# Accumulating DMAs from GpSimd, column-tiled projections and earlier Q steps in a kernel of softmax and linear attention

## The chip, the cores and the metric

The kernel runs on one core of one Trainium2 chip. The metric is device time in microseconds. Three runs of the kernel before gave 707.06, 707.91 and 708.15 us, median 707.91. Profiles come from one further execution of each kernel. Engine names are those of the profile: PE is TensorE, ACT is ScalarE, DVE is VectorE, POOL is GpSimd, SP is SyncE, PEld is the loading of weights into TensorE.

## What is computed

The input `x` has 2048 rows of 512 columns. Branch A is softmax attention with 32 heads of 16 columns, branch B is linear attention with the same sizes, and a gate mixes them by row:

```python
qkv = x @ wqkv                                   # each branch has its own weights
# A, for each of 32 heads
p = softmax(q @ k.T * 16**-0.5);  a = (p @ v) @ wo_A
# B
pq, pk = phi(q), phi(k)                          # phi(t) = where(t > 0, t + 1, exp(t)) + 1e-6
b = ((pq @ (pk.T @ v)) / (pq @ sum(pk) + 1e-6)) @ wo_B
g = sigmoid((x * gate_w).sum(-1))
out = g * a + (1 - g) * b
```

Nearly all of the time goes into A: 32 heads x 2048 x 2048 exponentials.

## The kernel before

**Rounds and units.** The 32 heads are four groups of eight (`t8`), the 2048 queries four chunks of 512 (`qc`). A pair of both is worked in two rounds, even heads and odd heads, so there are 32 rounds of four heads. A unit is one head's scores of 128 keys against 512 queries: one matmul with 32 rows (`Qpad`, `KT`, row tiles of TensorE), whose result fills one PSUM bank. A round has 16 key blocks x 4 heads = 64 units, the kernel 2048.

**ScalarE's way.** Two or three units make a score group. Their matmuls (L1821) fill up to three banks, and one exponential (L1836, on ACT) turns them into probabilities in the buffer `PT`. Two sets of three banks take turns, so TensorE fills one while ScalarE empties the other. The values are then gathered by matmuls with 32 columns (`pv_cols`, L1235): four of them, one per head and column tile, are a set and add to the accumulator's bank.

**VectorE's way.** VectorE takes over some units ("claims", L1417). It reads the bank (L1430), shifts the score into an integer of 16 bits, and these bits, read as a float of 16 bits, are a rough power of two. Three such patterns, shifted by the constants in `STEPS` (0, 342, 683) and weighted by `WEIGHTS`, add up to an approximation of the exponential. Up to four units share a buffer of `DP` and are a bundle. When it is full (`close_tri`, `try_close`, L1440 to L1461), VectorE writes the two further patterns into two further buffers of `DP`, one addition of 128x2048 each (L1461). The weights stand in scaled copies of V, kept for key blocks from `KB2` on (L831). A claimed unit thus costs 686 ns of VectorE for its bank, a quarter of two additions, and three matmuls of values instead of one.

**The rest.** Projections for Q, K and V (`proj_pieces`, L745; `step_Q`, L793), all of branch B (`step_M` L908 and its neighbours), the output projections (`out_fns` L1015, `step_pre` L1035, `step_out` L1061) are "steps" in chains, each cut into pieces of two matmuls. A step of Q ends in eight DMAs of 16 KB from `Qs` into `Qpad` (`fill_q`, L781), issued by SP.

**What sets the order.** A planner in Python writes the order when the kernel is built. It keeps an estimated clock for each engine, with durations written down as constants, and places one score group after another (L1775 on). Between two groups it puts sets of values, a piece of a step that is due (`misc_step`, L1614; a step's `target` is counted in three units of ScalarE's way), or a claim; where TensorE would idle, it adds a warm-up matmul on zeros (`fill`, L1639). `MARGIN` is how far ahead of ScalarE a score group is to be ready. A change of TensorE's tiling (row tiles, column tiles, whole array) counts as `SWITCH_T` (L569). Every engine works its list strictly in order and waits on semaphores of the engine or DMA that it depends on. The last round gathers its values in another way, with probabilities as the stationary operand (52 columns a matmul).

Of the kernel before, what the change touches and what calls it, by code (L numbers as in the profile page):

```python
# [17 lines left out]
STATS = {}  # L18
# [10 lines left out]
WEIGHTS = (1.0, 203 / 256, 161 / 256)  # L29
STEPS = (0, 342, 683)  # L30
NG4 = len(STEPS)
# [22 lines left out]
HINT_AT = 150  # L54
KB2 = 10

# [144 lines left out]
def bass_gated_mix__mha_block__linear_attn_block__prompt_kernel(  # L201
# [20 lines left out]
    NPT = 20  # L222
    NB = 13
    NQS = 4
# [4 lines left out]
    KV0, KV1 = 1.0, 1.2  # L229
    PRE_T = 3  # L230
    PRE_GAP = 6
    OUT_GAP = 6

    with ExitStack() as es:
# [52 lines left out]
        xn0 = PT[:, 9 * 512:9 * 512 + 4 * D].rearrange("p (b c) -> p b c", b=4)  # L287
        NTU = 512 * NTRI

        DP = SB([128, NB, NTU], BF16, "DP")  # L290
# [65 lines left out]
        out_counts = [0] * NOUTT  # L356
        semQ = [SEM(f"s_q{i}") for i in range(NQS)]
        q_counts = [0] * NQS

# [136 lines left out]
        def pump(now, look=0.25):  # L496
            try_close()
            while items and DV.t <= now + look:
# [12 lines left out]
                if best[2] > now + look + WAIT_BANK:  # L511
                    return
                emit_item_op(best[1])
# [91 lines left out]
        def f_mm(o, l, r, start=True, stop=True, sg=False):  # L605
            return lambda: nc.tensor.matmul(o, lhsT=l, rhs=r, start=start, stop=stop, skip_group_check=sg)  # L606

        def f_tr(o, i):
            return lambda: nc.tensor.transpose(o, i, identb[:])  # L609
# [108 lines left out]
        def run_piece(b, piece, first):  # L718
            fns, reads, dur, mac = piece
            pe_macro(fns, reads=reads, writes=[r_bank[b]], dur=dur, mac=mac)  # L720

# [186 lines left out]
        def step_M(c, **kw):  # L908

            rd = [r_xcol[c % 2]] + phi_res  # L910

            def pieces(b):
                o = bank_ap(b)
                fns = [f_mm(o, xcol[c % 2][:, tb, :], phi_of(tb)[0], start=(tb == 0), stop=(tb == NTB - 1)) for tb in range(NTB)]
                return [(fns[j:j + 2], rd, 2 * MM512, 2 * MM512) for j in range(0, NTB, 2)]
# [98 lines left out]

        def out_fns(o, tb, which, last=True):  # L1015
            fns = []
            for n, (kind, i) in enumerate(which):
                l = OT[:, i, 128 * tb:128 * (tb + 1)] if kind == "A" else obt(tb)[:, i, :]
                fns.append(f_mm(o, l, (woA if kind == "A" else woB)[:, i, :], start=(n == 0), stop=(last and n == len(which) - 1)))
            return fns  # L1020
# [14 lines left out]
        def step_pre(k, last=True, **kw):  # L1035
            tb = 4 * (NQC - 1) + k
            rd = [r_OT[t][NQC - 1] for t in range(NT8 - 1)] + [r_OBT[tb], r_woA, r_woB, r_g]

            def pieces(b):
                fns = out_fns(bank_ap(b), tb, order_out[:-1], last=last)  # L1040
                return [(fns[j:j + 2], rd, len(fns[j:j + 2]) * MM512, len(fns[j:j + 2]) * MM512) for j in range(0, 7, 2)]
# [19 lines left out]
        def step_out(tb, **kw):  # L1061
# [3 lines left out]
            def pieces(b):  # L1065
                fns = out_fns(bank_ap(b), tb, order_out)
                return [(fns[k:k + 2], rd, 2 * MM512, 2 * MM512) for k in range(0, 8, 2)]

# [159 lines left out]

        PT_URGENT = 12

# [4 lines left out]
        def pv_cols(now, r, force, want, most, least):  # L1235
# [59 lines left out]
        def pv_step(now, force=False, want=None, most=3, least=4):  # L1295

            r = acc_round[0]
            if r >= NR:
# [83 lines left out]

        MIN_LEFT = 14
        MIN_LEFT_LAST = 20
# [24 lines left out]
        def free_buffers():  # L1409

            used = [e[3] for e in pv_pending]
            held_ = [c[0] for c in (tri[0], closing[0]) if c is not None]
            free = [i for i in range(NB) if i not in held_ and not any(x.pend or x in used for x in r_DP[i])]
            free.sort(key=lambda i: max(x.tr for x in r_DP[i]))
            return free

        def claim(r, u, b, beside, in_group=False):  # L1417
            taken[r].add(u)
            if tri[0] is None:
                ntri[0] += 1  # L1420
                tri[0] = (free_buffers()[0], [])
# [15 lines left out]
        def add_products(i, z, k, r, u):  # L1437
            pv_pending.append((r, u, [(DP[:, i, 512 * k:512 * (k + 1)].bitcast(F16), z)], r_DP[i][k], Fraction(1, NG4)))

        def close_tri():  # L1440
# [26 lines left out]

        GPR = 15.8
        B0 = 0.8
        B1 = 24  # L1470
        chains = []
# [13 lines left out]
        for qc in range(1, NQC):  # L1485
            st = step_Q(0, qc)
            st.cond = (lambda qc=qc: act_round[0] > r_of(0, qc) - 3)
            st.target = GPR * (r_of(0, qc) - 2) + 4
            a_chain.append(st)
        all_seqs = []  # L1490
        for t8 in range(1, NT8):
# [8 lines left out]
            for t in range(NQC):  # L1500
# [15 lines left out]
                st.cond = after_qk(r_of(t8, t) - 3)  # L1516
                st.target = GPR * (r_of(t8, t) - 2) + 4
                seqs.append(st)
# [95 lines left out]
        def misc_step(now, t_late):  # L1614

            if hold[0] is not None:
                if now + hold[0][2][0][2] > t_late:
                    return False
# [9 lines left out]
            if due is not None and (c is None or load > STARVE or cur_g[0] > due[0].target + late() or hurry()):  # L1628
                if now + 0.43 > t_late:
                    return False  # L1630
# [8 lines left out]
        def fill(now):  # L1639

            r_acc = r_bank[acc_bank[0]]
            if acc_n[0] == 0 or r_acc.pend:
                if hold[0] is None or not hold[0][0].spare or hold[0][3]:
# [5 lines left out]
                return True  # L1649
            pe_macro([f_mm(acc_of(acc_bank[0]), warm[:], warm4, start=False, stop=False, sg=True)], reads=[r_warm],  # L1650
                     writes=[r_acc], dur=MM512, mac=0.216)
# [6 lines left out]
        MOST = 3  # L1658
        ROOM = 0.4
        CLAIM_LOAD = 3.2  # L1660
        LATE_CLAIM = 4.0
        STARVE = 6.0
        MAC_LOW = 0.47
        MAC_END = 0.45
        FILL_T = 0.2
        FILL_AHEAD = 0.7
        END_FROM = 44
        RING_LOAD = 4
        RING_LATE = 4
        BEHIND = 30  # L1670
        LEND = 110
        RES_FROM = 60
        MARGIN = 0.19
        PV_LAG = 14
        LATE = 9
        LAG_END = 12
# [199 lines left out]

        while tri[0] is not None or closing[0] is not None:
            close_tri()
            if closing[0] is not None and not pv_step(PE.t, force=True):
                flush_items()  # L1880
# [241 lines left out]
```

## Time and profile before

| | us |
|---|---|
| median of three runs | 707.91 |
| the profiled execution | 707.36 |
| its span, first to last instruction | 705.5 |
| first exponential of the scores starts | 9.18 |
| busy TensorE / VectorE / ScalarE | 678.4 / 659.4 / 691.4 |
| busy GpSimd, all in the first 10 us | 8.4 |
| SBUF-to-SBUF and other DMAs on SP's queue | 20.12 MB |

The span is what the profile's rows add up to; the profiled execution took 1.9 us more than its span, the median 2.4 us more. A group of the profile is read as: line, engine, operation, output from input, shapes, count, busy us and mean ns, idle time ahead of it and what ended it. Nearly all matmuls are recorded at L606, a helper, so they are told apart by their tiles: `Qpad,KT` are scores, `PT,Vaug` values of ScalarE's units, `DP,Vaug` values of VectorE's units, `warm` the fillers. TensorE's busy time is not its load, since matmuls are pipelined and each record of one lasts longer than the distance to the next.

### The profile page before, as it was taken

What the parts mean: (1) busy time and instruction counts of PE and PEld (TensorE: products, weight loads), DVE (VectorE), ACT (ScalarE), POOL (GpSimd) and SP (SyncE); (2) the same over time, 40 slices, a digit from 0 to 9 for tenths busy, and PEclk for the clock granted to TensorE, in tenths of its full rate; (3) what the DMA queues carried; (4) which work ended last, traced back from release to release, by engine and by line L of the source; (5) the groups of instructions that cost most, each with busy time, mean ns of one, the idle gap of its engine ahead of it and who ended that gap; (6) DMA issues with size and microseconds to landing.
All of it is one profiled execution on the core that took longest, in us unless ns stands there. A gap on an engine that the chain in (4) does not pass through costs nothing.

```text
span 705.5 us, 17061 instructions
## 1 busy us (share of the span) xinstructions
PE 678.4 (96%) x6734; PEld 207.3 (29%) x6734; DVE 659.4 (93%) x1140; ACT 691.4 (98%) x712; POOL 8.4 (1%) x19
## 2 busy tenths in 40 slices
PE   8999999999999999999999999999999999999997
PEld 4322222332222322222222223233222232222235
DVE  4799999999999999997899999999999999999992
ACT  6999999999999999999999999999999999999996
POOL 4000000000000000000000000000000000000000
PEclk9999999999999999999999999999999999999999
DMA  9800101010010101111010020100102031010111
GB/s 224 221 9 10 25 1 33 2 25 10 9 24 2 25 10 39 25 31 25 9 26 8 2 41 17 32 6 18 35 17 47 9 48 34 22 47 25 43 23 35
DMA packets 44811, 22.83 MB, mean 32 GB/s; under 512 B 33976, under 2 KB 40568, under 8 KB 44728
## 3 DMA queue, kind: packets, MB, share of 16 engines
q1 hardware_dynamic: 42712, 20.12, 12.9%
q10 hardware_dynamic: 2016, 1.57, 0.9%
q8 instruction: 56, 0.92, 0.5%
q14 instruction: 27, 0.22, 0.1%
HBM read 8.00 MB, written 2.10 MB: 14 GB/s over the span
## 4 chain that ended last, share of the span: by engine, by line
PE 44%; ACT 41%; issue 12%; DVE 3%; ACTq 0%; POOL 0%; POOLq 0%
PE ps L606 43%; ACT PT L1836 39%; ACT epool L881 2%; DVE DP L1430 1%; DVE DP L1461 0%; PE ps L609 0%; DVE xT L1732 0%; DVE KT L774 0%; DVE DP L1932 0%; DVE Vaug L829 0%; DVE oraw L1202 0%; ACTq L2045 0%; DVE OBT L886 0%; DVE rraw L1178 0%; DVE dev L1152 0%
## 5 line engine op out<-in xcount | busy, mean ns | idle before, releaser
L1836 ACT ACTIVATE PT<-ps 128x1024 bf16<-128x1024 f32 (+1 forms) x672 | 682.9, 1339 | 1.6 <-PE ps L606 1.4
L1430 DVE TENSOR_SCALAR DP<-ps 128x512 int16<-128x512 f32 x576 | 381.6, 686 | 13.7 <-PE ps L606 9.3
L606 PE MATMUL ps<-Qpad,KT 32*128 32x512 bf16 x2048 | 268.6, 384 | 19.4 <-ACT PT L1836 13.8
L1461 DVE TENSOR_SCALAR DP<-DP 128x2048 int16<-128x2048 int16 x288 | 192.4, 685 | 0.0
L606 PE MATMUL ps<-DP,Vaug 128*32 128x512 f16 x1680 | 181.9, 385 | 0.2
L606 PE MATMUL ps<-PT,Vaug 128*32 128x512 bf16 x1424 | 165.9, 385 | 0.4 <-DVE oraw L1202 0.4
L606 PEld LDWEIGHTS ps<-Qpad,KT 32*128 32x128 bf16 x2048 | 66.9, 91 | 270.8 <-ACT PT L1836 245.8
L606 PEld LDWEIGHTS ps<-DP,Vaug 128*32 128x32 bf16 x1680 | 44.0, 94 | 62.9 <-issue 35.6
L606 PE MATMUL ps<-warm 128*128 128x512 bf16 (+1 forms) x173 | 59.7, 397 | 1.1 <-POOL warm L650 1.1
L606 PEld LDWEIGHTS ps<-PT,Vaug 128*32 128x32 bf16 x1424 | 39.5, 94 | 57.2 <-issue 45.2
L606 PE MATMUL ps<-xT,wA 128*128 128x512 bf16 x108 | 32.3, 384 | 0.0
L881 ACT ACTIVATE epool<-ps 128x512 bf16<-128x512 f32 x32 | 26.8, 836 | 0.0
L606 PEld LDWEIGHTS ps<-warm 128*128 128x128 bf16 x173 | 14.0, 99 | 30.5 <-issue 28.5
L1202 DVE COPY oraw<-ps 128x512 f32<-128x512 f32 x31 | 21.2, 684 | 0.1
L606 PE MATMUL ps<-woA,OT 128*128 128x512 bf16 x64 | 18.9, 383 | 0.0
L606 PE MATMUL ps<-xT,wB 128*128 128x512 bf16 x64 | 18.7, 384 | 0.0
L606 PE MATMUL ps<-wB,xT 128*128 128x512 bf16 x64 | 18.7, 383 | 0.0
L886 DVE SCALAR_TENSOR_TENSOR phi<-ps,epool 128x512 bf16<-128x512 f32 x24 | 16.4, 682 | 0.0
L774 DVE CAST KT<-ps 128x512 bf16<-128x512 f32 (+1 forms) x16 | 10.6, 662 | 4.6 <-PE ps L606 4.6
L606 PE MATMUL ps<-wA,xT 128*128 128x128 bf16 x192 | 14.7, 220 | 0.0
L829 DVE CAST Vaug<-ps 128x512 bf16<-128x512 f32 x16 | 11.0, 685 | 3.6 <-PE ps L606 3.6
L606 PEld LDWEIGHTS ps<-wA,xT 128*128 128x128 bf16 x192 | 10.8, 98 | 5.4 <-issue 5.0
(98 smaller groups left out, 240.4 us busy)
## 6 DMA issues: line engine op xcount, KB each, us to landing
rbc<-oraw SPq DMA_DIRECT2D x16, 256.0 KB
OT<-in_A_x_dram SPq DMA_DIRECT2D x4, 512.0 KB, 8.2
Qpad<-Qs SPq DMA_DIRECT2D x124, 16.0 KB, 1.8
oraw<-oraw SPq DMA_DIRECT2D x60, 32.0 KB, 1.9
wA<-in_A_wqkv_dram SPq DMA_DIRECT2D x1, 1536.0 KB, 7.7
wB<-in_B_wqkv_dram SPq DMA_DIRECT2D x1, 1536.0 KB, 9.0
out_dram<-outt SPq DMA_DIRECT2D x12, 128.0 KB, 1.8
phi<-in_A_x_dram ACTq DMA_DIRECT2D x3, 256.0 KB, 6.3
```

The lines of the kernel that those rows point to most:

```text
L606: return lambda: nc.tensor.matmul(o, lhsT=l, rhs=r, start=start, stop=stop, skip_group_check=sg)
L774: push(1, [(lambda: nc.vector.tensor_copy(KT[:, par, c0:c1], src), [r_bank[b]], [r_KT[par][t]], d_psum(n), None)])
L829: ops = [(lambda: nc.vector.tensor_copy(v_group(NQC * par + v)[:, :, :, 0:16], src), [r_bank[b]], [r_V[par][v]], d_psum(512), lambda: v_do ...
L881: op(AC, lambda: nc.scalar.activation(epool[:, s, :], bank_ap(b), ACT.Exp), reads=[r_bank[b]], writes=[r_e[s]], dur=0.6, issue=0.48)
L886: (lambda: nc.vector.scalar_tensor_tensor(out=dst, in0=bank_ap(b), scalar=0.0, in1=epool[:, s, :], op0=ALU.max, op1=ALU.add), [r_bank[b], ...
L1202: push(0, [(lambda: nc.vector.tensor_copy(oraw[:, half, :], acc), [r_acc], [r_oraw[half]], d_psum(512), evicted)])
L1430: push(0 if in_group else 1, [(lambda: nc.vector.tensor_scalar(DP[:, i, 512 * k:512 * (k + 1)].bitcast(I16), bank_ap(b), FRAC - Y_BIAS4, Y ...
L1461: push(3, [(lambda z=z, i2=i2, y=y, n=n: nc.vector.tensor_single_scalar(DP[:, i2, 0:n].bitcast(I16), y, STEPS[z], ALU.add), r_DP[i][0:len( ...
L1836: op(AC, lambda p0=p0, b0=b0, n=n: nc.scalar.activation(PT[:, 512 * p0:512 * p0 + n], ps[:, 512 * b0:512 * b0 + n], ACT.Exp, scale=LN2 / F ...
```

## The change

The bundles of VectorE's way get a second way to their patterns. When a bundle is closed and `can_grow` allows it (all units of one round, not the last round, enough of the round left, few others under way), it becomes a "grown" bundle: VectorE makes no further pattern. Once all matmuls that read the present pattern are placed, `grow` has GpSimd issue a DMA that adds a buffer filled with 342 (`plus`) to the bundle's own buffer, in place; the next pattern's matmuls wait for its semaphore, and this is done twice. The buffers needed fall from three to one for such a bundle, the third constant becomes 684 for both ways, and `DP` has 12 buffers instead of 13. In the build 118 DMAs do this for 59 bundles.

Matmuls of 128 output columns in the projections, in `step_M` and in most output projections become four column tiles each (`f_cols`), so that they run in the tiling of the values. Steps of Q are due four counts earlier (`Q_OFF`). Scaled copies of V are kept from key block 8 on instead of 10. A dozen numbers of the planner change.

```diff
-STEPS = (0, 342, 683)
+STEPS = (0, 342, 684)
-KB2 = 10
+KB2 = 8
-    NB = 13
+    NB = 12
-    PRE_T = 3
-    PRE_GAP = 6
+    PRE_T = 5
+    PRE_GAP = 8
...
+        plus = SB([128, NTU], BF16, "plus")
+        op(PO, lambda: nc.gpsimd.memset(plus[:].bitcast(I16), STEPS[1]), writes=[r_plus], dur=4.0)
...
+        def f_cols(o, l, r, start=True, stop=True):
+            return [f_mm(o[32 * j:32 * j + 32, :], l[:, 32 * j:32 * j + 32], r, start=start, stop=stop, sg=True) for j in range(4)]
...
-                    fns = [f_mm(o, l_of(cc), r_of(cc), start=(cc == 0), stop=(cc == NCC - 1))
-                           for cc in range(c0, c0 + split)]
-                    out_.append((fns, reads, split * MM512 * max(n, 128) / 512, split * MM512 * n / 512))
+                    fns = [f for cc in range(c0, c0 + split)
+                           for f in f_cols(o, l_of(cc), r_of(cc), start=(cc == 0), stop=(cc == NCC - 1))]
+                    out_.append((fns, reads, split * MM512 * max(n, 128) / 512, split * MM512 * n / 512, "cols"))
...
+            if grown:
+                g_res = {x for it in grown for x in r_DP[it[0]]}
+                rest = [e for e in rest if e[3] in g_res] + [e for e in rest if e[3] not in g_res]
...
-        MIN_LEFT = 14
+        MIN_LEFT = 24
+        GROW_LEFT = 30
+        GROW_MAX = 3.0
+        GROW_NEXT = 2.5
+        GROW_T = 2.6
+        GROW_ISSUE = 1.0
+        GROW_LAT = 1.5
...
+        def can_grow(us):
+            rs = {r for r, u in us}
+            if len(rs) > 1:
+                return False
+            r = rs.pop()
+            if r >= NR - 1 or (r == act_round[0] and left(r) < GROW_LEFT):
+                return False
+            todo = sum(NG4 - 1 - it[2] for it in grown) + max(0.0, dma_free[0] - PE.t) / GROW_T
+            return todo <= (GROW_MAX if r == acc_round[0] else GROW_NEXT)
+
+        def grow():
+            for it in list(grown):
+                i, us, z = it
+                used = [e[3] for e in pv_pending]
+                if any(x in used or x.pend for x in r_DP[i][0:len(us)]):
+                    continue
+                if z == NG4 - 1:
+                    grown.remove(it)
+                    continue
+                it[2] = z = z + 1
...
+                dst, src, cnt = DP[:, i, 0:n].bitcast(I16), plus[:, 0:n].bitcast(I16), p_counts[i]
+                res = r_DP[i][0:len(us)]
+                st = max(est_start(PO, [r_plus], res), PO.t)
+                begin = max(st + GROW_ISSUE, dma_free[0])
+                dma_free[0] = begin + GROW_T * len(us) / NTRI
+                lands = dma_free[0] + GROW_LAT
+                ev = PO.add(lambda dst=dst, src=src: nc.gpsimd.dma_start(dst, src, accum_op=ALU.add),
+                            _deps_for([r_plus], res), inc=False, dma_sem=semP[i])
...
         def close_tri():
+            if tri[0] is not None and can_grow(tri[0][1]):
+                grown.append([*tri[0], 0])
+                tri[0] = None
...
+        Q_OFF = 0
-        GPR = 15.8
+        GPR = 15.2
-            st.target = GPR * (r_of(0, qc) - 2) + 4
+            st.target = GPR * (r_of(0, qc) - 2) + Q_OFF
...
-        CLAIM_FREE = 3
+        CLAIM_FREE = 1
+        OVER = 0.15
-        CLAIM_LOAD = 3.2
-        LATE_CLAIM = 4.0
+        CLAIM_LOAD = 3.5
+        LATE_CLAIM = 3.7
-        MARGIN = 0.19
+        MARGIN = 0.15
```

More of the change, by code (lines that the diff above doesn't have):

```diff
@@ L357, in bass_gated_mix__mha_block__linear_attn_block__prompt_kernel @@
         semQ = [SEM(f"s_q{i}") for i in range(NQS)]
+        semP = [SEM(f"s_p{i}") for i in range(NB)]
+        p_counts = [0] * NB
         q_counts = [0] * NQS
@@ L718, in run_piece @@
         def run_piece(b, piece, first):
-            fns, reads, dur, mac = piece
-            pe_macro(fns, reads=reads, writes=[r_bank[b]], dur=dur, mac=mac)
+            fns, reads, dur, mac = piece[:4]
+            pe_macro(fns, reads=reads, writes=[r_bank[b]], dur=dur, mac=mac, mode=piece[4] if len(piece) > 4 else "full")
         def start_step(step, b):
@@ L913, in pieces @@
                 o = bank_ap(b)
-                fns = [f_mm(o, xcol[c % 2][:, tb, :], phi_of(tb)[0], start=(tb == 0), stop=(tb == NTB - 1)) for tb in range(NTB)]
-                return [(fns[j:j + 2], rd, 2 * MM512, 2 * MM512) for j in range(0, NTB, 2)]
+                fns = [f_cols(o, xcol[c % 2][:, tb, :], phi_of(tb)[0], start=(tb == 0), stop=(tb == NTB - 1)) for tb in range(NTB)]
+                return [(fns[j] + fns[j + 1], rd, 2 * MM512, 2 * MM512, "cols") for j in range(0, NTB, 2)]
             def post(b):
@@ L1012, in step_num, with out_fns @@
             return Step(pieces, post, reads=rd, **kw)
-        def out_fns(o, tb, which, last=True):
+        def out_fns(o, tb, which, last=True, cols=False):
             fns = []
@@ L1018, in out_fns @@
                 l = OT[:, i, 128 * tb:128 * (tb + 1)] if kind == "A" else obt(tb)[:, i, :]
-                fns.append(f_mm(o, l, (woA if kind == "A" else woB)[:, i, :], start=(n == 0), stop=(last and n == len(which) - 1)))
+                fns.append((f_cols if cols else f_mm)(o, l, (woA if kind == "A" else woB)[:, i, :], start=(n == 0),
+                                                      stop=(last and n == len(which) - 1)))
             return fns
@@ L1039, in pieces @@
             def pieces(b):
-                fns = out_fns(bank_ap(b), tb, order_out[:-1], last=last)
-                return [(fns[j:j + 2], rd, len(fns[j:j + 2]) * MM512, len(fns[j:j + 2]) * MM512) for j in range(0, 7, 2)]
+                fns = out_fns(bank_ap(b), tb, order_out[:-1], last=last, cols=last)
+                mode = "cols" if last else "full"
+                fns = fns if last else [[f] for f in fns]
+                return [(sum(fns[j:j + 2], []), rd, len(fns[j:j + 2]) * MM512, len(fns[j:j + 2]) * MM512, mode) for j in range(0, 7, 2)]
             def post(b):
@@ L1411, in free_buffers @@
             used = [e[3] for e in pv_pending]
-            held_ = [c[0] for c in (tri[0], closing[0]) if c is not None]
+            held_ = [c[0] for c in (tri[0], closing[0], *grown) if c is not None]
             free = [i for i in range(NB) if i not in held_ and not any(x.pend or x in used for x in r_DP[i])]
@@ L1418, in claim @@
             taken[r].add(u)
+            if tri[0] is not None and tri[0][1][0][0] != r and can_grow(tri[0][1]):
+                close_tri()
             if tri[0] is None:
@@ L1616, in misc_step @@
             if hold[0] is not None:
-                if now + hold[0][2][0][2] > t_late:
+                if now + (SWITCH_T if pe_mode[0] == "full" else 0.0) + hold[0][2][0][2] > t_late + OVER:
                     return False
@@ L1628, in misc_step @@
             if due is not None and (c is None or load > STARVE or cur_g[0] > due[0].target + late() or hurry()):
-                if now + 0.43 > t_late:
+                if now + FIRST_T > t_late + OVER:
                     return False
@@ L1649, in fill @@
                 return True
-            pe_macro([f_mm(acc_of(acc_bank[0]), warm[:], warm4, start=False, stop=False, sg=True)], reads=[r_warm],
-                     writes=[r_acc], dur=MM512, mac=0.216)
+            if pe_mode[0] == "cols":
+                fns = [f_mm(acc_of(acc_bank[0])[32 * j:32 * j + 32, :], warm[:, 0:32], warm4, start=False, stop=False, sg=True) for j in range(4)]
+                pe_macro(fns, reads=[r_warm], writes=[r_acc], dur=SET_T, mac=0.216, mode="cols")
+            else:
+                pe_macro([f_mm(acc_of(acc_bank[0]), warm[:], warm4, start=False, stop=False, sg=True)], reads=[r_warm],
+                         writes=[r_acc], dur=MM512, mac=0.216)
             STATS["fills"] = STATS.get("fills", 0) + 1
@@ L1874, in bass_gated_mix__mha_block__linear_attn_block__prompt_kernel @@
             g += 1
-        while tri[0] is not None or closing[0] is not None:
+        while tri[0] is not None or closing[0] is not None or grown:
             close_tri()
-            if closing[0] is not None and not pv_step(PE.t, force=True):
+            grow()
+            if (closing[0] is not None or grown) and not pv_step(PE.t, force=True):
                 flush_items()
```

37 lines of the change are left out of this document (27 added, 10 removed).

## The prediction

> **What bounds the kernel now.** I read the page's busy shares first, then ScalarE's waits, then the timelines of ScalarE and TensorE, then the DMA issues.
>
> ```profile
> PE 678.4 (96%) x6734; PEld 207.3 (29%) x6734; DVE 659.4 (93%) x1140; ACT 691.4 (98%) x712; POOL 8.4 (1%) x19
> ...
> PEclk9999999999999999999999999999999999999999
> ```
>
> Three engines look full, and the clock is granted in every slice. ScalarE is the fullest. ScalarE's list of waits says how little it stands still inside the loop:
>
> ```profile
> ACT DP L1926 <- PE ps L606: 3.6, 1, 3.6
> ...
> ACT PT L1836 <- PE ps L606: 1.4, 3, 0.5
> ```
>
> The exponential (L1836) stood still for 1.4 us in all; the 3.6 us come after the last one. (A group that is only late shows as starts further apart, below.) A recorded exponential overlaps the next, so its price is taken from starts in ScalarE's timeline (start, length, instruction, count):
>
> ```profile
> 38.65 6.64 ACT L1836 ACTIVATE PT<-ps 128x1024 bf16<-128x1024 f32 x7
> 44.98 0.80 ACT L881 ACTIVATE epool<-ps 128x512 bf16<-128x512 f32 x1
> 45.46 6.25 ACT L1836 ACTIVATE PT<-ps 128x1536 bf16<-128x1536 f32 x6
> ...
> 683.53 13.82 ACT L1836 ACTIVATE PT<-ps 128x1536 bf16<-128x1536 f32 x10
> ...
> 691.52 5.83 ACT L1836 ACTIVATE PT<-ps 128x1536 bf16<-128x1536 f32 x4
> ```
>
> Seven two-unit groups take 44.98 - 38.65 = 6.33 us, 0.904 each; the small exponential of the linear branch takes 45.46 - 44.98 = 0.48; at the end six three-unit groups take 691.52 - 683.53 = 7.99, 1.332 each. The forms of L1836 are counted in the groups kept apart by shape:
>
> ```profile
> L1836 ACT ACTIVATE PT<-ps 128x1024 bf16<-128x1024 f32 x544 | 535.1, 1260 | 0.5 <-PE ps L606 0.4
> L1836 ACT ACTIVATE PT<-ps 128x1536 bf16<-128x1536 f32 x128 | 201.8, 1678 | 1.1 <-PE ps L606 1.0
> ```
>
> 544 x 0.904 + 128 x 1.332 + 32 x 0.48 = 677.7 us, of the 688.2 us from the first exponential (9.18) to the end of the last (691.52 + 5.83 = 697.35). So ScalarE's own work is the time, with some 10 us of late score groups, 9.2 us before it and 8.2 us behind it.
>
> **ScalarE: what it loses.** In the build of the changed kernel L1916 (the same exponential) has 572 two-unit and 97 three-unit groups: 572 x 2 + 97 x 3 = 1435 units instead of 1472. That is 31 x 1.332 = 41.3 less and 28 x 0.904 = 25.3 more: **-16.0 us**.
>
> **VectorE: why it can take 37 units more.**
>
> ```profile
> L1430 DVE TENSOR_SCALAR DP<-ps 128x512 int16<-128x512 f32 x576 | 381.6, 686 | 13.7 <-PE ps L606 9.3
> L1461 DVE TENSOR_SCALAR DP<-DP 128x2048 int16<-128x2048 int16 x288 | 192.4, 685 | 0.0
> ```
>
> 613 evictions instead of 576 cost 37 x 0.686 = +25.4; 188 full additions and 2 short ones instead of 288 full ones save about 99 x 0.685 = -67.8. VectorE does 42 us less in a span some 10 us shorter, so it has more room than now, and evictions should free banks no later.
>
> **TensorE: does it keep up?** Its timeline shows the price of a set and of a change of tiling:
>
> ```profile
> 640.84 0.39 PE L606 MATMUL ps<-PT,Vaug 128*32 128x512 bf16 x1
> ...
> 641.07 0.39 PE L606 MATMUL ps<-PT,Vaug 128*32 128x512 bf16 x3
> 641.39 0.39 PE L606 MATMUL ps<-Qpad,KT 32*128 32x512 bf16 x3
> ```
>
> Set follows set in 0.22-0.23 us (640.84 to 641.07); from column tiles to row tiles it is 0.32, so a change costs 0.095. Over the whole trace a whole 128x512 matmul follows another in 0.226 and a set of four column tiles another in 0.216, so the rewritten projections cost no more. In the build the order of matmuls has 1366 changes of tiling instead of 1474: 108 x 0.095 = -10.3 us. Without the warm-up fillers the array work is even: 306 us before and after, counted by these prices, as 24 more sets of values (827, not 803) stand against cheaper projections. Fillers, which only stand in idle time, go from 155 to 131, some 6 us. So 10.3 + 6 us go away against 16 on ScalarE: TensorE keeps pace, with 131 x 0.22 = 29 us of spare left. If that cover were gone, a late score group would delay ScalarE one for one. The margins of the order are cut too (MARGIN 0.19 to 0.15, OVER 0.15): between 0 and 669 x 0.04 = 27 us; the row nearest is today's loss of 10 us at 0.19, of which 0.04/0.19 is 2: **+2**.
>
> **The tail.** Behind the last score group the order has 184 matmuls of 52 columns instead of 128, and three projections more. In the tail's timeline 72 such matmuls take 1.97 us, 25 ns each: 56 x 0.025 + 3 x 0.22 = 2.1; and the last exponential, which covers them, is a two-unit one, 0.43 shorter: **+2.5**.
>
> **Q sooner.** The step (its projection, one eviction by VectorE, then eight DMAs of 16 KB on SP) is due 4 counts of three units, 4 x 1.33 = 5.3 us, earlier. Nothing of it is added. On SP it can pass the DMAs of a normalisation, at some 0.6 us an issue; their reader (L1178) waited for none of them today, and TensorE for no Qpad DMA: 0, and a few of L1178's late starts if that cover is gone.
>
> **The DMAs.** 118 of them, two each for 59 bundles, 512 KB each. Each waits on POOL for TensorE's last read of the pattern, and TensorE, later, for its landing; behind a waiting matmul stand all score groups, so ScalarE waits. The trace shows no accumulating DMA and none issued by POOL. The nearest rows:
>
> ```profile
> Qpad<-Qs SPq DMA_DIRECT2D x124, 16.0 KB, 1.8
> ...
> PT<-in_A_x_dram ACTq DMA_DIRECT2D x1, 512.0 KB, 4.1
> ```
>
> The fixed part is at most 1.8 us. The packets of the second row are 4096 B, 0.164 us each in the trace, 8 for each of 16 DMA engines: 1.3 us a pass. Low end 1.8 + 1.3 = 3.1 (the old content costs nothing); high end two passes at the first slice's 224 GB/s, 1.05 MB / 224 = 4.7, so 6.5. I take two passes at the packet's price, 1.8 + 2.6 = 4.4, nearest to the 4.1 of the same size, and allow up to 5 for POOL's issue. Now the room: in the build's order there are, between the point where the DMA may go and the first matmul that reads its result, 4 score groups in 4 cases, 5 in 23, 6 in 34, 7 in 22, 8 in 22, 9 in 10 and 10 in 3; a group lasts (572 x 0.904 + 97 x 1.332) / 669 = 0.97, with the others about 0.99 us. Landing in 4.4 us is short in 4 cases by 0.44; in 5 us, by 4 x 1.04 + 23 x 0.05 = 5.3. Where two bundles go together the second lands one transfer later, and those have the 8 groups and more. **+2**, between 0 and 34 (6.0 us, below).
>
> POOL and VectorE may also hold each other up. L1461 handles 2048 elements in the 685 ns in which L1430 handles 512 from PSUM, so it runs in a faster mode. No row has it beside busy POOL (POOL's work ends at 9.6 us, L1461 starts at 31). Bounds: 0, and on TensorE's side 118 x 19% (188 x 0.685 of 690) x 0.34 (half of one) = 8 us late, on VectorE's side 118 issues x 0.27 additions per us x 0.64 (SP's longest issue row, of rbc) squared = 13 us on an engine with 70 idle. I take 0 in the sum.
> The Trainium skill, SBUF — State Buffer, section "SBUF: two separate sides", speaks against the change here: while VectorE runs in a two-port mode GpSimd cannot write the descriptors of its DMAs, and the first to start blocks the other for a whole instruction; no run here shows it yet.
>
> **Sum.** -16.0 + 2.5 + 2 + 2 = -9.5 us, against the profiled execution's own 707.36 (span 705.5): 697.9. The median of the runs is 0.55 higher than that execution; I give 698.
>
> **Rivals.**
> *Landing later than the order allows* (slower). If a lone DMA lands after 6.0 us, 4 are short by 2.04, 23 by 1.05 and 34 by 0.06: 34 us, so 707.4 - 11.5 + 34 = 730; at 6.5 us 65, so 761. It decides from about 5.2 us, where 4 x 1.27 + 23 x 0.28 = 11.5 us eat the whole gain. For it: POOL's issue is unmeasured, each round trip is serial, TensorE has only 29 us of spare. Against: packets of 0.164 us, DMA engines idle (tenths 0 or 1). Chance 0.23.
> *POOL and VectorE block each other*: the 8 and a part of the 13 us come, about 704-712, middle 707. For it: VectorE's fast additions are 19% of the time. Against: two thirds as many as now. Chance 0.13.
> *Nothing is lost*: margins and DMAs cost 0, 707.4 - 13.5 = 693.9 or, with a tail as now, 691. Chance 0.14.
> *It doesn't do what it says*: the exponentials saved stand in the build, so that can't be; folded into the first rival.
> *My forecast*: 694-704, chance 0.50.
>
> **How the numbers follow.** About 0.2%, 1.4 us, is what a measurement of this kernel can tell from no change. Faster: 0.50 + 0.14 + 0.05 of the blocking case = 0.69; same 0.05; slower 0.23 + 0.03 = 0.26. The range from 691 to 724 leaves out little below and some 0.15 of the first rival above.
>
> **What would show it.** Right: L1916 at 572 and 97 with starts 0.904 and 1.332 apart; ScalarE's busy share still 98%; TensorE waiting for DMAs on DP by less than 10 us; a landing of 4-5 us. Wrong: a wait of TensorE for such a DMA of tens of us (first rival); L1534 or POOL's issues far longer than 685 and 640 ns (second); score groups late by more than 15 us with no DMA behind them (margins).

## The result and the profile after

The changed kernel takes **804.57 us** (median of 4, 801.57 to 806.49) against 707.88 (707.06 to 708.15): 1.1366 times as long (1.1352 to 1.138). The prediction was 698.0, range 691 to 724. Ratios here leave out executions more than 1.5% above the fastest of their kernel, so for a kernel whose times spread they are a little below the quotient of the medians, and traffic (below) has one such execution left and no ratio.

The page's busy shares, granted clock, DMA share and chain of waits:

```profile
PE 710.9 (89%) x8235; PEld 213.1 (27%) x8235; DVE 631.3 (79%) x1079; ACT 688.9 (86%) x709; POOL 119.2 (15%) x138
...
PEclk9999899997999986999997989999898898989989
DMA  9656354575543744457554646655467647745531
...
PE 40%; DMA 37%; DVE 14%; issue 4%; ACT 3%; SPq 1%; POOL 0%; DVEq 0%; ACTq 0%; POOLq 0%
PE ps L611 39%; DMA DP<-plus 21%; DMA rbc<-oraw 8%; DVE DP L1455 7%; DMA oraw<-rraw 5%; ACT PT L1916 3%; DVE DP L1534 2%; DMA rsum<-oraw 2%; DMA oraw<-oraw 1%; SPq L560 1%; DVE oraw L1215 1%; DVE OT L1205 1%; DVE phi L896 0%; POOL DP L1498 0%; DVE KT L784 0%
```

No engine is full any more: ScalarE fell from 98% to 86%. DMA holds 37% of the chain, and not only by the new DMAs: `rbc`, `oraw<-rraw` and `rsum` are the small DMAs of a normalisation. Before, the row of the DMA engines was this; behind the first two slices three slices show more than one tenth:

```profile
DMA  9800101010010101111010020100102031010111
```

ScalarE's work itself is what the prediction counted (groups kept apart by shape):

```profile
L1916 ACT ACTIVATE PT<-ps 128x1024 bf16<-128x1024 f32 x572 | 548.9, 1080 | 90.7 <-PE ps L611 89.0
L1916 ACT ACTIVATE PT<-ps 128x1536 bf16<-128x1536 f32 x97 | 139.9, 1535 | 4.4 <-PE ps L611 4.1
```

572 and 97 groups, but with 93 us of waiting for TensorE where there were 1.4. Who makes TensorE late is in the list of waits (us in total, times, longest):

```profile
ACT PT L1916 <- PE ps L611: 93.1, 91, 5.7
...
PEld ps L611 <- DMA DP<-plus: 51.5, 60, 4.5
DVE OT L1205 <- DMA rbc<-oraw: 48.3, 12, 6.5
...
PE ps L611 <- DVE DP L1455: 35.7, 14, 5.6
PE ps L611 <- DMA DP<-plus: 33.5, 37, 4.2
...
DVE rraw L1191 <- DMA rsum<-oraw: 5.9, 3, 2.3
```

There are two kinds. TensorE waits for patterns that have not landed (`DP<-plus`). And VectorE, which waited for no DMA of a normalisation before, stands 54 us for `rbc` and `rsum`. The multiply that reads `rbc`, before and then after (the last figures are the idle time ahead of it and what ended it):

```profile
L1192 DVE TENSOR_TENSOR OT<-oraw,rbc 128x512 bf16<-128x512 f32 x15 | 10.2, 683 | 0.0
```

```profile
L1205 DVE TENSOR_TENSOR OT<-oraw,rbc 128x512 bf16<-128x512 f32 x15 | 10.4, 690 | 51.1 <-DMA rbc<-oraw 48.3
```

The bank evictions queued behind that instruction are late, and so TensorE waits for L1455. The DMA issues (KB each, median us from issue to landing), after and then before, show what became of small transfers:

```profile
DP<-plus POOLq DMA_DIRECT2D x118, 512.0 KB, 5.5
...
Qpad<-Qs SPq DMA_DIRECT2D x124, 16.0 KB, 2.3
oraw<-oraw SPq DMA_DIRECT2D x60, 32.0 KB, 4.2
...
out_dram<-outt SPq DMA_DIRECT2D x12, 128.0 KB, 5.7
```

```profile
oraw<-oraw SPq DMA_DIRECT2D x60, 32.0 KB, 1.9
...
out_dram<-outt SPq DMA_DIRECT2D x12, 128.0 KB, 1.8
```

One stop, read from the timelines of SP, POOL, VectorE, TensorE and ScalarE (start, length, instruction, count, idle before it):

```profile
262.72 8.45 SPq L560 DMA_DIRECT2D Qpad<-Qs  x8
271.28 1.89 SPq L560 DMA_DIRECT2D oraw<-rraw  x2
274.79 0.64 SPq L560 DMA_DIRECT2D rbc<-oraw  x1
```

```profile
266.64 0.84 POOL L1498 DMA_DIRECT2D DP<-plus  x1 [6.25 <-PE ps L611]
267.99 0.86 POOL L1498 DMA_DIRECT2D DP<-plus  x1 [0.51 <-PE ps L611]
```

```profile
269.23 4.86 DVE L1455 TENSOR_SCALAR DP<-ps 128x512 int16<-128x512 f32 x8
279.96 0.69 DVE L1205 TENSOR_TENSOR OT<-oraw,rbc 128x512 bf16<-128x512 f32 x1 [5.87 <-DMA rbc<-oraw]
```

```profile
273.68 0.39 PE L611 MATMUL ps<-Qpad,KT 32*128 32x512 bf16 x3
...
281.40 0.61 PE L611 MATMUL ps<-Qpad,KT 32*128 32x512 bf16 x3 [5.65 <-DVE DP L1455]
```

```profile
282.05 1.02 ACT L1916 ACTIVATE PT<-ps 128x1024 bf16<-128x1024 f32 x1 [5.68 <-PE ps L611]
```

Two accumulating DMAs go out at 266.6 and 268.0 into eight Qpad issues that take SP 8.45 us; `oraw<-rraw` gets its turn at 271.28, `rbc` at 274.79. VectorE has run out of work that stands ahead of L1205 and waits 5.87 us, two evictions behind it come late, TensorE stops for 5.65 us and ScalarE for 5.68. The stop has a tail: the clock record of the trace grants 0.5 from 277.9 to 288.1 us, and the score matmuls behind the stop last 0.61 us instead of 0.39. Over all normalisations, from the eviction of `oraw` to the start of L1205, the trace has a median of 14.2 us before and 19.0 after.

### The profile page after: what moved, and what is told of

Its sections match the earlier page's. It is cut to its first block, busy times and chain, and to the rows that moved or that the text cites. A ratio compares the mean times of both kernels' runs of the same rounds, so it can differ in the third digit from the quotient of the medians.

```text
span 802.5 us, 20316 instructions
## 1 busy us (share of the span) xinstructions
PE 710.9 (89%) x8235; PEld 213.1 (27%) x8235; DVE 631.3 (79%) x1079; ACT 688.9 (86%) x709; POOL 119.2 (15%) x138
## 4 chain that ended last, share of the span: by engine, by line
PE 40%; DMA 37%; DVE 14%; issue 4%; ACT 3%; SPq 1%; POOL 0%; DVEq 0%; ACTq 0%; POOLq 0%
PE ps L611 39%; DMA DP<-plus 21%; DMA rbc<-oraw 8%; DVE DP L1455 7%; DMA oraw<-rraw 5%; ACT PT L1916 3%; DVE DP L1534 2%; DMA rsum<-oraw 2%; DMA oraw<-oraw 1%; SPq L560 1%; DVE oraw L1215 1%; DVE OT L1205 1%; DVE phi L896 0%; POOL DP L1498 0%; DVE KT L784 0%
## 5 line engine op out<-in xcount | busy, mean ns | idle before, releaser
L1455 DVE TENSOR_SCALAR DP<-ps 128x512 int16<-128x512 f32 x613 | 401.1, 683 | 67.4 <-PE ps L611 64.8
L611 PE MATMUL ps<-Qpad,KT 32*128 32x512 bf16 x2048 | 287.4, 406 | 40.9 <-DVE DP L1455 35.5
L611 PE MATMUL ps<-DP,Vaug 128*32 128x512 f16 x1800 | 202.8, 403 | 34.8 <-DMA DP<-plus 32.5
L1498 POOL DMA_DIRECT2D DP<-plus x118 | 108.0, 961 | 643.3 <-PE ps L611 566.1
L1534 DVE TENSOR_SCALAR DP<-DP 128x2048 int16<-128x2048 int16 (+1 forms) x190 | 126.8, 680 | 0.4 <-PE ps L611 0.3
L611 PE MATMUL ps<-warm 128*32 128x512 bf16 (+2 forms) x316 | 56.3, 416 | 1.1 <-POOL warm L659 1.1
L1205 DVE TENSOR_TENSOR OT<-oraw,rbc 128x512 bf16<-128x512 f32 x15 | 10.4, 690 | 51.1 <-DMA rbc<-oraw 48.3
L611 PE MATMUL ps<-xT,wA 128*32 128x512 bf16 x432 | 33.8, 406 | 0.2
L611 PE MATMUL ps<-wB,xT 128*32 128x512 bf16 x256 | 21.1, 418 | 3.1 <-DVE phi L896 3.1
L611 PE MATMUL ps<-xT,wB 128*32 128x512 bf16 x256 | 20.3, 397 | 0.0
L611 PE MATMUL ps<-woA,OT 128*32 128x512 bf16 (+1 forms) x226 | 19.3, 400 | 0.0
```

The costliest lines, as they stand in the source:

```text
L1205: push(1, [(lambda: nc.vector.tensor_tensor(OT[:, t8, 512 * qc:512 * (qc + 1)], oraw[:, 0, :], rbc[:], ALU.mult), [r_oraw[0], r_rbc], [r_O ...
L1455: push(0 if in_group else 1, [(lambda: nc.vector.tensor_scalar(DP[:, i, 512 * k:512 * (k + 1)].bitcast(I16), bank_ap(b), FRAC - Y_BIAS4, Y ...
L1498: ev = PO.add(lambda dst=dst, src=src: nc.gpsimd.dma_start(dst, src, accum_op=ALU.add), _deps_for([r_plus], res), inc=False, dma_sem=semP[i])
L1534: push(3, [(lambda z=z, i2=i2, y=y, n=n: nc.vector.tensor_single_scalar(DP[:, i2, 0:n].bitcast(I16), y, STEPS[z], ALU.add), r_DP[i][0:len( ...
```

## The experiments

Two theories, with experiments chosen to part them. **L** (landing): TensorE stands at its wait for an accumulating DMA. **S** (shared engines): the accumulating DMAs delay the small DMAs of the normalisations, and VectorE, which works in order, stands for them. Against both stood **T**: the other parts of the change, or the issue on GpSimd, cost the time.

**small_dma** (the same order, hardly any data):

```diff
-nc.gpsimd.dma_start(dst, src, accum_op=ALU.add)
+nc.gpsimd.dma_start(dst[:, 0:32], src[:, 0:32], accum_op=ALU.add)
```

> The changed kernel's instructions in the changed kernel's order, but each of GpSimd's 118 DMAs adds only 32 of its 2048 columns (the addition on the other columns is left out). Waits, issues and column tiles stay, the traffic goes from 62 MB to 1 MB. Theory L (TensorE stands at the wait for a landing that comes later than the order allows) and theory S (the traffic holds up the small DMAs of normalisation, VectorE stands for them in order and evicts banks late) both say 694 to 702 us, the sum of the prediction without its DMA term. Theory T (column tiles, cut margins, or GpSimd's issue itself) says 760 us or more.

Measured 695.35 us (695.02 to 696.17), ratio 0.9827 (0.981 to 0.9843). T falls: the order with all 118 issues is faster than before when hardly anything has to be moved.

```profile
PE 670.5 (97%) x8235; PEld 207.4 (30%) x8235; DVE 627.4 (90%) x1079; ACT 675.7 (97%) x709; POOL 121.9 (18%) x138
```

GpSimd is as busy as in the changed kernel, and ScalarE and TensorE are full.

**no_grow** (no bundle is ever grown; the planner orders the rest anew: `if len(rs) > 0: return False` in `can_grow`) and **only_cols** (the kernel before with nothing but `f_cols` and its callers):

> The changed kernel with no grown bundle: VectorE makes all patterns, the planner orders anew; column tiles, margins and Q times stay. L and S: between 698 and 712 us, since VectorE again has the additions and ScalarE its units. T: above 740 us.

> The kernel before with nothing but the column tiles of the projections (576 claimed exponentials, 672 groups, no accumulating DMA, no GpSimd work). All theories: within 1% of before, 702-713 us. Below 700 the columns alone would be a gain that I put at nothing, above 715 a loss that my sum lacks.

712.48 us, ratio 1.008 (1.0056 to 1.0103), and 713.15, ratio 1.0079 (1.0062 to 1.0096). Both are half a us or less above what I had expected. Without grown bundles neither version gains; what the change can gain needs them.

**traffic** (the kernel before, with DMAs of the same kind onto a buffer that nobody reads, so that no matmul can wait for them):

```diff
+            if g >= 30 and g % 11 in (0, 5) and p_count[0] < 118:
+                deps = [_Ev(AC, AC.n), r_plus.w] + ([_Raw(semP, 16 * p_count[0])] if p_count[0] else [])
+                p_count[0] += 1
+                PO.add(lambda: nc.gpsimd.dma_start(plus[:].bitcast(I16), plus[:].bitcast(I16), accum_op=ALU.add), deps, inc=False, dma_sem=semP)
```

> The kernel before, order of TensorE, VectorE, ScalarE and SP unchanged, and GpSimd issues 117 accumulating DMAs of 512 KB (zeros added to a buffer of their own), one for about every 5.5 score groups; nobody waits for them. L: 707 to 710 us. S: 725 to 760 us, with VectorE waiting for DMAs on rsum and rbc, which it does not do before.

767.79 us (752.51 to 773.95): **60 us in the median, 45 in the fastest of four executions, from traffic that no instruction of the kernel uses**. The median lies above S's 725 to 760. The waits in an execution of 766.84 us:

```profile
ACT PT L1841 <- PE ps L610: 51.7, 57, 4.4
...
DVE OT L1197 <- DMA rbc<-oraw: 34.7, 12, 4.6
...
DVE rraw L1183 <- DMA rsum<-oraw: 7.4, 6, 2.4
```

The same waits of VectorE as in the changed kernel (45 us in all, against 54), so S is real and is no consequence of L.

The packets' times in the traces say how thin the cover was. Before, the multiply starts 0.7 to 3.7 us (median 2.8) after the last packet of its `rbc`. From the end of the reciprocal to the issue of `rbc` it takes 3.8 us, from there to the last packet 4.0; with the traffic 6.7 and 6.0 (medians of 15 normalisations). That is 4.9 us more against a cover of 2.8, and in this trace the multiply starts less than 0.8 us after that packet every time.

**plain_copy** (`dma_start(dst, src)` without the addition, about half the work for the DMA engines, 0.161 us a packet instead of 0.339; the later patterns of grown bundles then hold only the constant):

> The changed kernel, but its DMAs write the constant over the pattern instead of adding it (the second and third pattern of grown bundles are then wrong), same size and order. One pass instead of two: a lone landing should fall from 4.5 to 4.9 us to about 3.1, a second of a pair from 7 to about 4.5. L: nearly all landings then fit, 698 to 712 us. S: half of the traffic is left, so about half of the loss, 740 to 755 us.

738.56 us, ratio 1.0439 (1.0404 to 1.0475). These DMAs land sooner (median 3.5 us), VectorE's wait for `rbc` is 27.7 us instead of 48.3: S goes with the traffic. The time is 1.4 us under S's range.

**norm_late, grow_late, both_late**: the changed kernel, its planner told longer times, so that the readers stand later in the order:

```diff
-            dma_batch(pairs, semN[k], reads, writes, n_counts[k], lands=N_LANDS[k])
+            dma_batch(pairs, semN[k], reads, writes, n_counts[k], lands=(N_SLOW if acc_round[0] < NR - 2 else N_LANDS)[k])
+        N_SLOW = [4.0, 4.0, 4.0, 5.0, 7.5]
...
-        GROW_T = 2.6
-        GROW_ISSUE = 1.0
-        GROW_LAT = 1.5
+        GROW_T = 3.2
+        GROW_ISSUE = 1.4
+        GROW_LAT = 1.2
```

The first half is norm_late, the second grow_late; both_late has both.

> The changed kernel, in which the planner is told that the landings of a normalisation take 4, 4, 4, 5 and 7.5 us instead of 2.7, 2.7, 2.7, 2.6 and 5.4, so that the reciprocals and multiplies stand later in VectorE's order (116 accumulating DMAs instead of 118). S (small normalisation DMAs delayed on the shared DMA engines, VectorE standing for them): the waits of L1205 and L1191 for rbc and rsum go from 54 us to under 12, the time to 735-755 us, and what is left is the waits for landed patterns. L (landings of the accumulating DMAs alone): 780 us or more, the waits for DP<-plus as before.

> The changed kernel, in which the planner is told that an accumulating DMA takes 1.4 + 3.2 + 1.2 us instead of 1.0 + 2.6 + 1.5 (one behind another one 3.2 us more), so that the score groups that read it stand later in TensorE's order (114 DMAs instead of 118, 603 claimed exponentials instead of 595). L: the waits of PE and PEld for DP<-plus fall from 85 us to under 25 and the time to 700-715 us. S: the traffic is nearly the same, so VectorE stands for rbc and rsum as before and the time is 755-770 us.

> Both of the planner's times changed together (116 DMAs, 595 claimed exponentials). If L and S are the whole loss, 705-720 us with the waits on both kinds of DMA under 20 us each; if something else takes time as well, 740 us or more.

770.76 us, ratio 1.0895 (1.0815 to 1.0975); 790.33, ratio 1.1162 (1.1142 to 1.1182); 748.39, ratio 1.0551 (1.0507 to 1.0595). The first two lie in neither theory's range of times, though the waits named went down as S and L had it; both_late came out in the range for "something else". norm_late first, then grow_late:

```profile
PEld ps L611 <- DMA DP<-plus: 61.0, 63, 4.5
...
DVE OT L1206 <- DMA rbc<-oraw: 6.3, 2, 5.2
```

```profile
DVE OT L1205 <- DMA rbc<-oraw: 62.4, 14, 8.1
...
PEld ps L611 <- DMA DP<-plus: 14.2, 20, 2.1
```

Each correction takes away its own wait, and the other one grows (51.5 to 61.0; 48.3 to 62.4), so neither theory's time could come true alone, and a wait's length does not say what its removal is worth. With both corrected 54 us of waits for patterns are left (PE's and PEld's added, which may overlap), where I had expected under 20.

**traffic_norm, traffic_norm2, norm_only**: the added traffic in a plan with later normalisations (N_SLOW as above; then 3.5, 3.5, 3.5, 4.5, 7.0 and only 100 DMAs), and that second plan with no traffic at all.

> The kernel before with 117 accumulating DMAs onto a buffer that nobody reads (767.79 us), and the planner told the later landings of a normalisation. S: only the place of VectorE's waits made those 60 us, so 708-722 us. If the traffic costs in another way (eviction, memory, clock by itself), 740 us or more.

> The kernel before, the same added traffic onto a buffer that nobody reads, but ended after 100 DMAs so that none is left behind the output (in the run of 741.06 us the last output was issued at 718.65 us and the added DMAs ran on to 741), and normalisation landings of 3.5, 3.5, 3.5, 4.5, 7.0 us in the plan. S: 710-722 us against 767.79, VectorE's waits for rbc and rsum under 10 us. If the traffic costs in another way: 735 or more.

> The order of the run of 715.64 us without its 100 added DMAs (the kernel before with normalisation landings of 3.5, 3.5, 3.5, 4.5 and 7.0 us in the plan). If S is all that the traffic does and the plan hides it, 711-716 us: the 8 us above before are then the price of the later normalisations. Under 709 if the traffic still costs time in that order.

741.06 us, ratio 1.046 (1.0426 to 1.0493), but there the last output was issued at 718.65 and only added DMAs ran on; 715.64, ratio 1.0116 (1.01 to 1.0133); 712.40, ratio 1.0076 (1.006 to 1.0093). **In an order that allows for them 100 of these transfers cost 3.2 us; in the order of before 117 cost 60 (45 in the fastest execution).** Fewer transfers are not the reason: in traffic_norm 113 went out before the last output, and that was issued 15.5 us later than before (718.65, not 703.14), the price of its order included. The 5 us between 707 and 712 are the price of norm_only's order.

**traffic_1k, after_1k**: each transfer cut into pieces of 512 columns, 1 KB a packet instead of 4 KB.

> The kernel before with the same added traffic as in the run of 767.79 us (117 x 512 KB onto a buffer nobody reads), but each transfer cut into four of 128 x 512 values, so packets of 1 KB instead of 4 KB. If a small normalisation DMA waits for one long packet per packet of its own on each engine (S at the level of packets), 715-730 us and the waits of VectorE for rbc and rsum under 15 us together. If the share of the engines' time is what counts, 755-770 us as with 4 KB.

> The changed kernel in the same order, each accumulating DMA cut into pieces of 1 KB packets (four issues instead of one on GpSimd, so the pattern lands later). S at the level of packets: the waits of VectorE for rbc and rsum (54 us) go under 15 us, and the waits of TensorE for landed patterns grow from 85 us to 100-150: 770-800 us. If the landings were nearly all of the loss, over 815 us; if the share of engine time counts, the waits for rbc stay at 40 us or more.

886.77 us, ratio 1.2556 (1.2524 to 1.2588), and 878.13, ratio 1.2387 (1.2335 to 1.2438). traffic_1k missed both its ranges, since I had left out GpSimd's issues: 468 keep it busy for 435 us. after_1k came out in its branch "over 815", for landings; but four issues in a row make each landing later, so this says little of the changed kernel. In traffic_1k the last output is issued at 716.4; the stretch from 720 on (PE, PEld, DVE, ACT, POOL busy; clock) holds added DMAs alone:

```profile
720.00:883.00 163.00, 0.00 (x0) 0.00 (x0) 0.00 (x0) 0.00 (x0) 90.48 (x104) 0.50 0.59 84
```

VectorE's wait for `rbc` is 11.2 us there instead of 34.7, and 7.3 in after_1k instead of 48.3. That speaks for S at the level of packets, but up to 700 us a sixth less traffic had been issued (356 quarters, not 107 wholes), so it is not shown cleanly. In after_1k TensorE pays for the late patterns: 141 us of waits of PEld and 121 of PE.

**half, half_late, both_late2, half_safe, half_safe2**: GROW_MAX and GROW_NEXT set to 0 and 0 (half, half_late), 1 and 1 (half_safe) or 0 and 0.5 (half_safe2), which leaves 60 DMAs; all but half with corrected times. both_late2 keeps 118 DMAs.

> The changed kernel with one grown bundle at a time (GROW_MAX and GROW_NEXT 0): 60 accumulating DMAs instead of 118, 595 claimed exponentials, no two DMAs together. If the loss goes with the traffic and pairs land worst (S and L): the waits of TensorE for landed patterns fall from 85 us to under 15, the waits for rbc and rsum to about half (20-30 us), the time 718-738. If only pairs matter: 695-705. If a single landing is the trouble: over 745.

> The same 60 DMAs, with both of the planner's times corrected: normalisation landings 3.5, 3.5, 3.5, 4.5, 7.0 us and accumulating DMAs 1.4 + 3.2 + 1.2 us (599 claimed exponentials). S and L together are the whole loss: 695-708 us, the waits on both kinds of DMA under 12 us each. If something else takes time beside the DMAs: 715 or more.

> All 118 DMAs with both of the planner's times corrected (normalisation 3.5, 3.5, 3.5, 4.5, 7.0 us up to six rounds before the end; 608 claimed exponentials against 595 in the run of 748.39 us). The pairs still land 6 to 9 us after their issue, which no setting here allows for: 735-760 us, with waits for landed patterns of 40-70 us. Under 720 if the end of the plan was what held the earlier run up.

> The changed kernel with 60 accumulating DMAs, normalisation landings of 4, 4, 4, 5, 7.5 us and accumulating DMAs of 1.4 + 3.4 + 1.6 us in the plan (594 claimed exponentials). S and L: the waits for landed patterns (17 us in the run of 711.92) and for rbc and rsum go under 6 us together, the time to 698-708 us: below before if the allowances are the only price. Over 712 if the later order itself costs what the waits gave back.

> As the run above with smaller allowances for the normalisation (3.5, 3.5, 3.5, 4.5, 7.0 us) and up to one bundle more behind the first (595 claimed exponentials): 698-710 us, with a few us more of waits for rbc and rsum.

| kernel | us | ratio (interval) | stops for a pattern | other stops |
|---|---|---|---|---|
| changed | 804.57 | 1.1366 (1.1352 to 1.138) | 12, 25.9 us | 14, 48.0 us |
| grow_late | 790.33 | 1.1162 (1.1142 to 1.1182) | 4, 6.8 | 19, 65.1 |
| norm_late | 770.76 | 1.0895 (1.0815 to 1.0975) | 18, 37.4 | 5, 13.6 |
| traffic | 767.79 | | none | 14, 40.7 |
| half | 755.70 | 1.0599 (1.0561 to 1.0636) | 7, 18.9 | 9, 21.4 |
| both_late | 748.39 | 1.0551 (1.0507 to 1.0595) | 8, 23.2 | 4, 10.5 |
| both_late2 | 741.00 | 1.0512 (1.0451 to 1.0574) | 3, 7.2 | 9, 23.3 |
| plain_copy | 738.56 | 1.0439 (1.0404 to 1.0475) | 7, 13.8 | 7, 17.3 |
| half_safe | 722.39 | 1.0198 (1.0169 to 1.0227) | 4, 9.0 | 4, 6.0 |
| half_safe2 | 712.19 | 1.0063 (1.0046 to 1.008) | 3, 5.6 | 1, 2.0 |
| half_late | 711.92 | 1.0063 (1.0041 to 1.0085) | 3, 7.8 | none |
| before, small_dma | 707.88, 695.35 | | none | none |

A stop is a place in TensorE's trace, behind 30 us, where two matmuls in a row start more than 1.2 us apart (sets follow in 0.22). The table answers what both_late had left open, whether a third thing takes time. **The loss goes with the stops**: over small_dma's 695.35 the changed kernel loses 109 us for 74 us of stops, both_late 53 for 34, both_late2 46 for 31, norm_late 75 for 51: 1.5 us for each us (grow_late 1.3). Where stops are few the quotient is higher, 1.8 for half_safe and 2.1 to 2.2 for half_late and half_safe2, where the order's own price (5 us in norm_only) weighs more. So what is left in both_late can be more of the same two waits; no run shows a third thing, and none excludes one. The lower clock is large enough for the rest: in the changed kernel the clock record has 20 stretches at 0.5, 117 us in all, of which 108 lie outside the stops (small_dma has 0.7 us). Half of 108 is 54 us, as a bound, for 35 us of loss beyond the stops. It was not separated from groups that are late by less than a stop.

Two expectations on pairs fell. half came out in its branch "over 745", that of single landings: no DMA has another one ahead of it there, and seven stops are still on patterns, as single DMAs land in 4.5 to 8.9 us (median 5.1) and these seven took 6.2 or more. Its waits for patterns are 51 us where I had under 15; those for `rbc` and `rsum` are 25, as expected. both_late2 lies in its range, but with 26 us of waits for patterns, not 40 to 70. And no version that makes all patterns beats the kernel before. half_late lies between its two branches. It still has 17 us of waits for patterns, and norm_only puts the price of its kind of order at 5 us; larger allowances did not help, since half_safe's order has eight stops again and half_safe2 stands where half_late does. half_safe landed in the branch "over 712", but its waits for patterns did not fall (20 us), so the reason given in that branch is not shown; half_safe2 is 2 us above its range.

## Why the prediction was wrong

- **ScalarE, -16.0: right**, and so is the sum without the DMAs: 707.4 - 16.0 + 2.5 + 2 = 695.9, and small_dma took 695.35. The terms hold one by one, but for a first exponential 0.7 us later: from the first exponential to the end of the last 688.2 us before, 674.1 in small_dma, 14.1 less where -16.0 + 2 was forecast. The tail too: from the end of the last exponential to the end of the trace 8.2 us before, 10.5 there. TensorE kept pace there, with 97% busy beside ScalarE's 97%.
- **VectorE, "evictions should free banks no later": failed, and by stops this is the larger part (48 of 74 us).** I weighed how much work VectorE has, not what its order waits for. It has less work than before (631.3 us for 659.4) and is late all the same, for 54 us of waits for `rbc` and `rsum` that before did not have. The cover that I never measured was 2.8 us in the median, and the traffic alone makes `rbc` 4.9 us later. No rival of mine had this mechanism.
- **Q sooner, "0": right without the traffic, wrong with it.** "Waited for none of them today" was true only of idle DMA engines, and I had counted one reader, the reciprocal (L1178, now L1191: 5.9 us), not the multiply, which has 48.3 of the 54. In small_dma the eight DMAs stand in the same place and L1205 waits 1.2 us in all (4.4 in no_grow). In the changed kernel SP's Qpad issues take 0.87 us on average instead of 0.63 (4.1 at most), and normalisations behind them start late; the time from the reciprocal to `rbc`'s issue is 3.8 us before, 4.0 in small_dma, 6.7 with the traffic alone and 7.0 after (medians); its 95th percentile is 9.0 with the traffic alone and 13.8 after. How many us the earlier Q costs in the changed kernel was not tried.
- **The DMAs, "+2": the price of one was nearly right, the room was not.** A packet takes 0.339 us, twice 0.164 as assumed, and a DMA with none ahead of it lands in 4.9 us (median of 42) where I took 4.4 and allowed 5. But 76 of the 118 are issued before the one ahead has landed, and take 6.2 us in the median and up to 9.9. "Those have the 8 groups and more" was wrong: 26 us of stops for patterns, 18 of them at ten DMAs of this kind. The other two stops are at lone ones that took 7.2 and 8.6, a spread that I had not allowed for either. This is the first rival, "landing later than the order allows", which I gave 0.23; its 730 us were only a part of what came.
- **POOL and VectorE blocking each other, 0: right.** small_dma has the same 118 issues beside the same additions and lost nothing. In the changed kernel VectorE's additions (L1534) take 680 ns where L1461 took 685. Single issues do stretch, from 0.84 us to 1.6 at most in the changed kernel. The Trainium skill, SBUF — State Buffer, section "SBUF: two separate sides", names this lock; stretched issues are all that the traces here show that could be it, and they cost no time.
- **The steps that failed, in short**: VectorE's "no later" and the "+2" of the DMAs. I compared the DMA engines' idle tenths with the DMAs' own work, and did not ask what the small transfers already in the loop would do beside them, nor how far landings spread. In their place stand 54 us of VectorE's waits and 26 us of TensorE's stops. The Trainium skill, DMA: Bandwidth & Descriptors, section "Issuing engines are not separate DMA queues", says that queues of different engines share the same 16 DMA engines. The runs agree: SP's 32 KB transfer went from 1.9 to 4.2 us.

## What to carry to other kernels

Before adding transfers, list the DMAs that some in-order engine already waits for or just misses waiting for, and ask what each does when it takes twice as long; low DMA use says nothing about that. Where an order is written out by a planner, a transfer's time is part of the order: added traffic cost 45 to 67 us in one order, and 100 of its 117 transfers 3 us in another. To price such a part, run it once with its data taken away (same issues, same order) and once with its traffic alone.

## What the runs showed of the hardware

- An accumulating DMA of 512 KB within SBUF, issued by GpSimd: issue 0.84 us, first packet 0.56 us later, then some 3.0 us; alone it lands in 4.9 us. A plain copy of the same size: issue 0.53, 1.6 us of packets, 3.1 us alone. With 64 bytes a packet: 2.2 us alone. Packets of 1 KB took 0.111 us, so four of them 0.44 where one of 4 KB took 0.339.
- Small transfers are delayed by waiting more than by slower packets: 2 KB packets on SP's queue have the same median, 0.158 us, before and after (mean 0.154 and 0.170), and 64-byte ones 0.011. The Trainium skill, DMA: Bandwidth & Descriptors, section "Queues, rings and completion order", has each DMA engine take turns between its queues packet by packet, which fits these rows; a packet of that page holds several descriptors, and no run shows whether it is a packet of the trace.
- SP's issues lengthen as well when the DMA engines are busy: its DMAs after 30 us took 188 us of issue before, 242 with the traffic alone and 254 after.
- The granted clock falls when TensorE stands still: 0.50 over 163 us without a matmul, 0.928 on average in the changed kernel, 1.0 in small_dma. The Trainium skill, TensorE: Matmul & The Clock Gate, section "What's actually happening", gives half rate for an idle TensorE, and the 0.50 agrees. What this adds to each stop was not separated from other late groups.
